# Splitting the first loads, adding filler matmuls in the opening, and turning the combine weights on VectorE in a fused attention and Soft-MoE kernel

## The chip, the cores and the metric

The kernel runs on one core of a Trainium2 chip. The metric is device time in microseconds (us) for one execution of the whole program, taken as a median of several runs. Lower is better. A core has TensorE (PE in the profile, with its weight loads as PEld), VectorE (DVE), ScalarE (ACT), GpSimd (POOL), and SyncE (SP), which here does nothing but issue transfers.

## The reference

The kernel computes two layers. The first is attention with 4 batches, 8 heads, 768 positions and head size 64, in which a query sees a key only where both fall into the same hash bucket. The bucket is given by the signs of six random projections.

```python
q_bits = einsum(q, proj) > 0          # 6 bits per query, the same for keys
mask   = bucket(q) == bucket(k)
scores = where(mask, q @ k.T / sqrt(64), -1e9)
attn   = exp(scores - scores.max(-1)); attn /= attn.sum(-1) + 1e-9
x      = (attn @ v) as [3072, 512]
```

The second is a Soft-MoE layer with 8 experts of 4 slots each, hidden size 1024.

```python
logits     = x @ phi                              # [3072, 32]
d          = softmax over the 3072 positions;  slot_input = d.T @ x
h          = relu(slot_input[e] @ w1[e]);      slot_out[e] = h @ w2[e]
c          = softmax over the 32 slots
out        = c @ slot_out                         # [3072, 512]
```

Everything is float32; the weights `w1` and `w2` are 64 pieces of 512 KB, and the output is 12 pieces of 512 KB.

## The kernel before

**Attention, head by head.** Heads go in pairs that share a 128-row tile of raw values. `load` brings q and k of a pair, `bits` projects them on TensorE and `over` compares with zero on VectorE. `split_hi` and `split_lo` cut each raw value into a rounded high part (ScalarE) and a remainder. `spread_y`, `spread_l`, `spread_x` and `spread_bits` move all that by transfers into the two operand tiles of a head, `Ys` and `Xs`, which lie together in `XYs` and of which there are three sets. Rows 64 to 96 hold the bits, scaled so that a mismatch costs a huge penalty. For each head the twelve steps of `smax` (L424, with a maximum on VectorE at L430 or L427) find a row maximum; `shift` and `shift_rows` (L445 to L459) turn it and send it by a small transfer into a row of `XYs`; the twelve steps of `scores` (L471, with an exponential on ScalarE at L475) then compute the probabilities; `acc` sums them on GpSimd and `av` (L500) multiplies with v.

**Order.** The order on every engine is written out beforehand. Each step gets a time in slots, six slots to a head, from the table `STEADY`, or from `ONCE` where it differs; `at` puts the steps into a plan, and they are emitted in the order of their times. An engine's queue, and the queue of transfers on SP, follow this order strictly.

**Opening.** The first head has functions of its own. SP issues the keys of the first pair (L228), the small tables, the queries (L230), `cst`, and v. `keep_warm` multiplies ones on TensorE (L264). `first_bits` (L380 to L392) computes the bits of both sides, copies raw rows into `Ys[0]` on ScalarE and compares on VectorE (`first_over`, L358, four pieces of 384 columns). `spin` (L438) is a filler matmul after each `smax` group of head 0. It reads 96 rows of `Ys[0]`. GpSimd clears rows 64 to 96 of `XYs` (L289), computes the remainders of the first pairs (L327) and compares the second head's bits (`bits_rest`).

**End of attention.** The last two heads have single-head versions (`one_sum` to `one_put`) of the normalization. `batch_max` to `batch_slots` fold each batch into the running softmax over positions. `batch_weigh` and `batch_share` make the combine weights `c` of a batch in the tile `call`.

**Experts.** `hidden` (L911) multiplies with w1, `above_zero` and `turned` (L917 to L927) apply the ReLU and transpose, `model` (L993) multiplies with w2 into the PSUM tiles `po0`, `po1` and `po2`, and `split_out` cuts the result into high and low parts. The weights arrive through pools `wa`, `wb`, `wy`, `wp`, `wl` and `wc`, which take over the memory of earlier stages as `free_pp`, `free_yp`, `free_ap`, `free_lp` and `free_mp` give it back (L855 to L878), and then through `wa` again once `hidden` has used its pieces. They are issued on SP at L198 and L200.

**Combine weights.** For the last product they must lie with the slots in rows. L941 and L942 split them into high and low parts; `arrange` (L944) copies three tiles of 128 positions at a time into a layout repeated four times, with eight small copies split between VectorE and GpSimd (L950); `turn_weights` (L953) transposes the three tiles by matmuls with the identity (L956) and copies them out of PSUM (L957). This is done eight times, between the steps of `hidden` and `model`.

**Output.** `send` (L1004) multiplies for one quarter of the 512 columns (128 columns) and all 3072 positions, in three pieces of 1024 positions (L1015), copies each out of PSUM (L1017) and issues its 512 KB (L1018). The first two quarters are sent after half of `po1`, the third between the halves of `po2`, the last at the end.

## Time and profile before

| What | Value |
| --- | --- |
| Median of 3 runs (lowest to highest) | 479.42 us (478.81 to 479.83) |
| The profiled execution's own time | 479.94 us |
| Its span, first to last instruction | 478.2 us |
| Busy share of the span: PE, DVE, POOL, ACT | 97%, 77%, 69%, 52% |
| Mean granted TensorE clock | 0.975 |
| HBM read, written | 52.76 MB, 6.29 MB |

The span is what the trace covers; 1.7 us of the profiled execution's time lie around it. Busy shares are averages over stages with different limits, so the views by stretch of time and the chain of waits decide what a change in one place is worth. The granted clock is 1.00 at full speed and 0.50 at half.

### The profile page before, as it was taken

How to read it: one execution, taken by the hardware profiler on the slowest of the kernel's cores; microseconds unless marked ns; L12 is line 12 of the kernel's file. 1: busy time of each engine (PE TensorE's matmuls, PEld its weight loads, DVE VectorE, ACT ScalarE, POOL GpSimd, SP SyncE). 2: the span in 40 equal slices, each digit the busy share in tenths (PEclk: the TensorE clock that was granted, in tenths of full speed). 3: DMA queues.
4: the chain of work that ended last, by engine and by line, in shares of the span. 5: the costliest groups of instructions: out<-in, count | busy, mean ns of one | idle time of the engine just before them, and what ended most of it. 6: DMA issues, size and time to landing. Idle time of an engine off the chain costs nothing.

```text
span 478.2 us, 10753 instructions
## 1 busy us (share of the span) xinstructions
PE 462.6 (97%) x4012; PEld 294.8 (62%) x4012; DVE 369.3 (77%) x690; ACT 247.5 (52%) x465; POOL 331.1 (69%) x236
## 2 busy tenths in 40 slices
PE   7899999999999999999999999999999999989992
PEld 4466666666666666666656666666656666553581
DVE  5649798989888888889898989898989865563242
ACT  4354646464657555555655555555654545431241
POOL 7758777878785978787868787878589888502200
PEclk9589999999999999999999999999999999999997
DMA  6667677767665757777674868584868479899967
GB/s 152 168 169 172 170 157 242 159 186 162 192 156 156 179 170 170 230 174 225 164 232 122 220 171 219 167 207 137 202 194 197 136 177 336 318 381 391 408 273 298
DMA packets 39697, 99.71 MB, mean 209 GB/s; under 512 B 7422, under 2 KB 13708, under 8 KB 39644
## 3 DMA queue, kind: packets, MB, share of 16 engines
q1 hardware_dynamic: 39260, 98.16, 70.9%
q0 software_dynamic: 224, 0.47, 0.5%
q8 instruction: 32, 0.52, 0.4%
q10 hardware_dynamic: 160, 0.39, 0.3%
q14 instruction: 21, 0.17, 0.1%
HBM read 52.76 MB, written 6.29 MB: 123 GB/s over the span
## 4 chain that ended last, share of the span: by engine, by line
PE 91%; DMA 4%; DVE 1%; SPq 1%; issue 1%; ACT 1%; DVEq 0%; ACTq 0%
PE st L471 29%; PE av L500 25%; PE smx L424 16%; PE qh L911 3%; PE mi L363 3%; PE mi L512 2%; PE mi L563 2%; PE mi L528 2%; PE qs L993 2%; DMA w<-w 2%; DMA out<-w 1%; PE mi L548 1%; DMA stage<-qk 1%; PE mi L718 1%; PE mi L455 1%; PE qa L956 1%
## 5 line engine op out<-in xcount | busy, mean ns | idle before, releaser
L488 POOL TENSOR_TENSOR acc<-acc,pt 128x768 f32<-128x768 f32 x125 | 229.0, 1832 | 9.6
L475 ACT ACTIVATE pt<-st 128x512 f32<-128x512 f32 x288 | 164.2, 597 | 65.0 <-PE st L471 59.9
L471 PE MATMUL st<-XY 128*128 128x256 f32 (+1 forms) x768 | 179.4, 349 | 0.1
L430 DVE TENSOR_REDUCE mx<-smx 128x1 f32<-128x512 f32 x192 | 131.0, 688 | 30.2 <-PE smx L424 27.5
L471 PEld LDWEIGHTS st<-XY 128*128 128x128 f32 x768 | 126.9, 191 | 18.3 <-ACT pt L475 1.7
L500 PE MATMUL av<-pt,v 128*32 128x384 f32 x1536 | 133.0, 486 | 0.0
L424 PE MATMUL smx<-XY 96*128 96x256 f32 (+1 forms) x384 | 120.8, 365 | 0.8 <-DVE mx L430 0.4
L482 POOL TENSOR_TENSOR acc<-pt 128x768 f32<-128x768 f32 x32 | 58.9, 1840 | 59.9 <-ACT pt L475 59.8
L500 PEld LDWEIGHTS av<-pt,v 128*32 128x32 f32 x1536 | 49.4, 110 | 72.8 <-issue 71.6
L424 PEld LDWEIGHTS smx<-XY 96*128 96x128 f32 x384 | 68.3, 195 | 30.1 <-issue 9.8
L427 DVE TENSOR_REDUCE mx<-smx 128x2 f32<-128x512 f32 x96 | 65.8, 686 | 6.5 <-PE smx L424 5.8
L504 ACT COPY avs<-av 128x384 f32<-128x384 f32 x32 | 15.3, 477 | 90.6 <-PE av L500 90.6
L324 DVE TENSOR_REDUCE stage<-stage 128x768 fp32r<-128x1536 f32 x28 | 49.0, 1785 | 0.0
L520 DVE RECIPROCAL rs<-sm 128x128 f32<-128x128 f32 x45 | 38.6, 914 | 11.9 <-ACT sm L515 7.0
L317 ACT ACTIVATE stage<-stage 128x768 fp32r<-128x768 f32 x30 | 24.1, 837 | 3.1 <-DMA stage<-qk 2.7
L565 DVE TENSOR_TENSOR xq<-mi,r 128x256 f32<-128x256 f32 x45 | 17.4, 413 | 1.5 <-PE mi L563 1.5
L950 POOL CAST avs<-lacc 128x48 fp32r<-128x48 f32 x8 | 2.1, 266 | 19.5 <-ACT lacc L941 12.4
L993 PE MATMUL qs<-w 128*32 128x128 f32 (+1 forms) x360 | 15.5, 305 | 0.0
L563 PE MATMUL mi<-ident,avs 128*128 128x128 f32 x90 | 14.7, 272 | 0.0
L911 PE MATMUL qh<-w,siT 128*32 128x512 f32 x128 | 14.6, 595 | 0.0
L563 PEld LDWEIGHTS mi<-ident,avs 128*128 128x128 f32 x90 | 11.7, 140 | 4.0
L363 PE MATMUL mi<-stage,pb 128*32 128x384 f32 x120 | 13.4, 521 | 0.0
(179 smaller groups left out, 330.1 us busy)
## 6 DMA issues: line engine op xcount, KB each, us to landing
w<-w SPq DMA_DIRECT2D x61, 512.0 KB
XY<-stage SPq DMA_DIRECT2D x62, 384.0 KB
stage<-qk SPq DMA_DIRECT2D x32, 384.0 KB
XY<-stage SPq DMA_DIRECT2D x62, 192.0 KB
v<-vt SPq DMA_DIRECT2D x32, 192.0 KB
out<-w SPq DMA_DIRECT2D x12, 512.0 KB
xq<-w SPq DMA_DIRECT2D x3, 512.0 KB
XY<-bt SPq DMA_DIRECT2D x62, 19.5 KB
```

The source lines that it names most:

```text
L324: nc.vector.tensor_reduce(out=w[:, 2 * x + 1], in_=stage[:, x:n + 1:n - x].rearrange("p t s -> p s t"), axis=AX.X, op=ALU.add, negate=True)
L424: nc.tensor.matmul(pt[:, o:o + b - a], Ys[h % N_Y][0:96, 0, t * P:(t + 1) * P], Ys[h % N_Y][0:96, 1, a:b], start=True, stop=True)
L427: nc.vector.tensor_reduce(out=mx[:, n - 1:n + 1], in_=pt.rearrange("p (a x) -> p a x", a=2), axis=AX.X, op=ALU.max)
L430: nc.vector.reduce_max(out=mx[:, n:n + 1], in_=pt, axis=AX.X)
L471: nc.tensor.matmul(pt[:, o:o + b - a], x[:, 1, i * P:(i + 1) * P], x[:, 0, a:b], start=first, stop=not first)
L475: nc.scalar.activation(pts[i // 2][:, 512 * u:512 * u + 512], pt, AF.Exp, scale=D ** -0.5)
L482: nc.gpsimd.tensor_tensor(out=s["acc"], in0=pr[:, 0:S], in1=pr[:, S:2 * S], op=ALU.add)
L488: eng.tensor_tensor(out=s["acc"], in0=s["acc"], in1=pr[:, a * S:(a + 1) * S], op=ALU.add)
L500: nc.tensor.matmul(s["av"][D * c + d:D * c + d + 32, 0:HC], s["v"][:, i, d:d + 32], pr[:, o + c * HC:o + (c + 1) * HC], start=(i == 0), st ...
L520: nc.vector.reciprocal(out=st[h]["rs"][:, k * P:(k + 1) * P], in_=st[h]["sm"][:, k * P:(k + 1) * P])
L563: nc.tensor.transpose(pt[:, o:o + P], st[h + a]["avs"][:, k * P:(k + 1) * P], ident)
L911: nc.tensor.matmul(ph[fh][32 * j:32 * j + 32], siT[:, k, 4 * g + j, :], wt[0, g, k, j][:, fh * 512:(fh + 1) * 512], start=(k == 0), stop=( ...
```

## The change

It has five parts.

1. **Raw values in halves.** The small table is loaded first; then the first 64 rows (head 0) of keys and queries, then the other 64 rows (head 1). The bits of head 0 are computed from its half alone, and `first_over` works in five pieces (512 columns once, 256 four times) instead of four of 384. The bits of both heads are computed again from all 128 rows (`more_bits`) for head 1. The second pair is loaded into the tiles `accs[1]` and `accs[2]`, early in the opening, and its `split_hi` and `bits` are early too. `cst` comes later. VectorE clears rows 64 to 96 of `Ys[0]` and a part of `Ys[2]`; GpSimd clears the rest and writes the row of ones directly, where transfers did it.
2. **Fillers.** `keep_warm` at the start becomes `spin(7)`, with 128 rows and 512 columns of a constant. Head 0's `smax` steps, but for the last tile of rows, are each followed by two (part 0) or one (part 1) fillers of 448 columns, 15 in all, where there were 9 of 512; six further steps `spin` of two fillers of 512 columns stand in the plan of the opening.
3. **Combine weights.** `batch_share` writes a high part and a remainder into a larger `call`. `combine` turns them by VectorE's 32 by 32 transpose, reading each block twice for the repeated layout: 16 instructions for each of three parts of 10, 8 and 6 tiles. `combine_round` copies a part on ScalarE. The first part stands in the plan beside heads 30 and 31, the second behind the first `hidden`, the third behind the second `turned`. `arrange`, `turn_weights` and the 24 matmuls with the identity are gone. The slot order of `phi`, `fold` and `siT` changes to suit.
4. **Outputs.** The first two quarters are sent in thirds, each third between parts of `po1`; the third quarter in two parts around the last half of `po2`.
5. **Pools and order.** `wb` has 7 buffers (5), `wy` 3 (6), `wc` 2 (1), and one more piece goes into the buffer of the first combine part. Scratch of `pair_rec` shares the buffer `dl`. All times in `STEADY` and `ONCE` are new, with separate entries for the first heads and for heads 29 to 31.

```diff
-N_WA, N_WB, N_WY, N_WP, N_WL, N_WC = 23, 5, 6, 3, 5, 1
+N_WA, N_WB, N_WY, N_WP, N_WL, N_WC = 23, 7, 3, 3, 5, 2
...
+    def raws(h, x):
+        return accs[1 + x] if h == 2 else raw[:, x]
...
+    def load_half(a):
+        for x in (1, 0):
+            nc.sync.dma_start(out=raw[D * a:D * a + D, x], in_=qk[x, 0, D * a:D * a + D])
...
-    load(0, (1,))
     nc.sync.dma_start(out=pre[:, 0:C_ID + 64], in_=first[:, 0:C_ID + 64])
-    load(0, (0,))
-    nc.sync.dma_start(out=pre[:, C_ID + 64:], in_=cst[:, C_ID:C_FD])
+    load_half(0)
+    load_half(1)
...
-    keep_warm(7, True)
+    def spin(n, cols=512):
+        pt = p_av.tile([P, 512], F32, name="av")
+        for _ in range(n):
+            nc.tensor.matmul(pt[:, 0:cols], idle[:, 0:P], idle[:, P:P + cols], start=True, stop=True)
+
+    spin(7)
...
+    nc.vector.memset(Ys[0][64:96].bitcast(F32), 0.0)
+    nc.vector.memset(Ys[2][64:96, 0].bitcast(F32), 0.0)
...
     def first_rows(i):
+        ts = XYs[i] if i else Xs[0]
+        if i == 2:
+            nc.gpsimd.memset(Xs[2][64:96, 0].bitcast(F32), 0.0)
+        nc.gpsimd.memset((ts[64:96, 1] if i == 2 else ts[64:96]).bitcast(F32), 0.0)
+        nc.gpsimd.memset(ts[ROW:ROW + 1, 1].bitcast(F32), 1.0)
...
+    def first_copy(x):
+        nc.scalar.copy(Ys[0][0:64, x], raw[0:64, x])
+
+    def first_bits(x):
+        first_pt[x] = p_st.tile([P, 512], F32, name="st")
+        for c, (a, b) in enumerate(((0, 512), (512, S))):
+            j = 2 * x + c
+            nc.tensor.matmul(first_pt[x][32 * j:32 * j + 32, 0:b - a], pb[0:D, 32 * x:32 * x + 32], raw[0:D, x, a:b],
+                             start=True, stop=True)
+
+    def more_bits():
+        pt = p_mi.tile([P, 512], F32, name="mi")
+        for x in range(2):
+            bits_of(0, x, pt)
+        st[0]["bt"] = st[1]["bt"] = pp.tile([P, HC], F32R, name="bt", bufs=1)
+        nc.scalar.copy(pts[0][:, 0:HC], pt[:, 0:HC])
...
-        if h == 0 and n % 4 != 1:
-            spin(1)
+        if h == 0 and t < NT - 1:
+            spin(2 - part, 448)
...
+        nc.scalar.copy(hb, cb)
+        eng.tensor_tensor(out=cb.bitcast(F32R), in0=cb, in1=hb, op=ALU.subtract)
+
+    cuts = 0, 10, 18, B * NT
+
+    def combine(n, j, q):
+        t0, t1 = cuts[n:n + 2]
...
+        src = tiles[32 * q:32 * q + 32, o:o + t1 - t0, j]
+        nc.vector.transpose(out=turned_shares[n][32 * j:32 * j + 32].rearrange("r (t q k) -> r t q k", q=4, k=32)[:, :, q],
+                            in_=src[:, :, None].broadcast_to([32, t1 - t0, 2, 4 * SPE]))
+
+    def combine_round(n):
...
+        nc.scalar.copy(cts[n // 2][:, o:o + t.shape[1]], t)
...
-    batch_weigh(B - 1)
-    batch_share(B - 1)
     ps_stack.close()
...
     hidden(hid[0], 0, range(KC))
+    batch_weigh(B - 1)
+    combine_some(1, 0, 8)
+    batch_share(B - 1)
+    combine_some(1, 8, 12)
     load_weights(wa, 10)
     hs0, hT0 = above_zero(hid[0])
-    cts = [piece().bitcast(F32R) for _ in range(B)]
     hidden(hid[1], 1, range(1))
     turned(hs0, hT0)
-    for k in range(1, KC):
-        hidden(hid[1], 1, range(k, k + 1))
-        more_weights(1)
+    combine_some(1, 12, 16)
+    combine_round(1)
+    hidden(hid[1], 1, range(1, KC))
...
     turned(hs1, hT1)
+    combine_some(2, 0, 16)
+    combine_round(2)
     model(po0, 0, 0, range(4, FC))
-    more_weights(1)
-    model(po0, 0, 1, range(4))
-    more_weights(1)
-    model(po0, 0, 1, range(4, FC))
+    model(po0, 0, 1)
     so0 = split_out(po0, 0)
-    more_weights(1)
     model(po1, 1, 0, range(4), left)
-    more_weights(1)
-    model(po1, 1, 0, range(4, FC), left)
-    more_weights(1)
-    send(so0[:, left], 0)
-    send(so0[:, right], 1)
-    model(po1, 1, 1, cols=left)
+    for n in range(3):
+        send(so0[:, left], 0, (n,))
+        send(so0[:, right], 1, (n,))
+        if n < 2:
+            model(po1, 1, n, range(4 - 4 * n, FC), left)
     so1 = split_out(po1, 1, left)
     po2 = po_tile(P)
     model(po2, 1, 0, cols=right)
-    send(so1, 2)
+    send(so1, 2, (0, 1))
     model(po2, 1, 1, cols=right)
-    send(split_out(po2, 1, right), 3)
+    so2 = split_out(po2, 1, right)
+    send(so1, 2, (2,))
+    send(so2, 3)
```

The new plan emits the opening in this order (steps of one kind drawn together): `first_bits(1)`, `first_copy(1)`, `first_hi(1)`, `load(2)`, `first_bits(0)`, `first_hi(0)`, `first_copy(0)`, the five `first_over` with `more_bits` and two `spin` steps among them, `spread_y(1)`, `split_hi(2)`, head 0's twelve `smax` with two `spin` steps among the last, `shift(0)`, `copy_ident`, `spin`, `bits(2)`, `spin`, `shift_rows(0)`, ten `smax` steps of head 1, and then the first `scores` of head 0. Before, six `smax` steps of head 1 had stood ahead of the first `scores`. Near the end of attention, `av(31, 0)` now stands ahead of `one_log`, `one_sum` and `one_turn` of head 30, which it followed before.

More of the change, by code (lines that the diff above doesn't have):

```diff
@@ new lines @@
+    ('scores', 1, 3, 0): 7.365414, ('scores', 1, 3, 1): 9.323528, ('scores', 1, 4, 0): 9.600144,
+    ('scores', 1, 4, 1): 8.023727, ('scores', 1, 5, 0): 8.410207, ('scores', 1, 5, 1): 7.791596,
+    ('shift', 0): -4.033776, ('shift', 1): 2.601141, ('shift_rows', 0): -2.144996, ('shift_rows', 1): 3.53153,
+    ('smax', 0, 0, 0): -6.352233, ('smax', 0, 0, 1): -8.6847, ('smax', 0, 1, 0): -8.289554,
+    ('smax', 0, 1, 1): -5.236389, ('smax', 0, 2, 0): -4.693721, ('smax', 0, 2, 1): -6.335023,
+    ('smax', 0, 3, 0): -5.871465, ('smax', 0, 3, 1): -9.069782, ('smax', 0, 4, 0): -9.552866,
@@ new lines @@
+    ('scores', 7, 2, 0): 42.260896, ('scores', 9, 2, 0): 54.260896, ('shift', 0): -26.571425,
+    ('shift', 1): 2.981046, ('shift', 2): 9.041854, ('shift', 31): 182.981046, ('shift_rows', 0): -15.952961,
+    ('shift_rows', 1): 4.460206, ('shift_rows', 2): 9.51256, ('shift_rows', 30): 177.51256,
+    ('shift_rows', 31): 184.460206, ('smax', 0, 0, 0): -69.826587, ('smax', 0, 0, 1): -59.319775,
+    ('smax', 0, 1, 0): -55.407906, ('smax', 0, 1, 1): -42.16177, ('smax', 0, 2, 0): -66.791397,
+    ('smax', 0, 2, 1): -55.145618, ('smax', 0, 3, 0): -52.669685, ('smax', 0, 3, 1): -36.552905,
@@ L220, in lsh_attention_soft_moe @@
     nc.vector.memset(ones, 1.0)
-    idle = pts[2][:, 0:P]
-    nc.vector.memset(idle, 1.0)
+    XYs = [held.tile([P, 2, 2, S], F32R, name=f"XY{i}") for i, held in enumerate((yp, lp, yq))]
+    Xs, Ys = [[t[:, :, n] for t in XYs] for n in range(2)]
+    idle = Xs[2][:, 0, 0:P + 512]
+    nc.vector.memset(idle.bitcast(F32), 1.0)
     eps = cp.tile([P, 1], F32, name="eps")
@@ L355, in first_x, with over @@
         nc.scalar.copy(Xs[0][0:64, x], st[0]["w4"][0:64, 3 * x])
-    def over(out, pt, rows, eng=nc.vector):
-        eng.tensor_scalar(out=out, in0=pt[rows, 0:HC], scalar1=con[rows, C_TH:C_TH + 1],
+    def over(out, pt, rows, eng=nc.vector, cols=slice(0, HC)):
+        eng.tensor_scalar(out=out, in0=pt[rows, cols], scalar1=con[rows, C_TH:C_TH + 1],
                           scalar2=con[rows, C_AM:C_AM + 1], op0=ALU.is_gt, op1=ALU.mult)
@@ L783, in at @@
         plan.append((when, len(plan), (f, *args)))
[L785 to L789 removed]
+    for i in range(N_Y):
         at(first_rows, i)
@@ L792, in lsh_attention_soft_moe @@
     at(load_phi)
-    at(keep_warm, 3, True, tag="a")
+    at(load_cst)
     at(copy_ident)
-    at(first_bits)
-    at(first_last)
+    for n in (1, 0):
+        at(first_copy, n)
+        at(first_bits, n)
+        at(first_hi, n)
+    for xab in ((1, 0, 512), (0, 0, 256), (1, 512, S), (0, 256, 512), (0, 512, S)):
+        at(first_over, *xab)
+    at(more_bits)
+    for n in range(6):
+        at(spin, 2, tag=n)
     at(bits_rest)
@@ L848, in lsh_attention_soft_moe @@
     at(keep_warm, 10, tag="c")
+    for j in range(4):
+        for q in range(4):
+            at(combine, 0, j, q)
+    at(combine_round, 0)
     last = NT * BH
```

351 lines of the change are left out of this document (171 added, 180 removed), and 5 rows, old and new, of the table ONCE.

## The prediction

> **What bounds the kernel now.** I read the page first: engine shares and the two rows over 40 slices.
>
> ```profile
> PE 462.6 (97%) x4012; PEld 294.8 (62%) x4012; DVE 369.3 (77%) x690; ACT 247.5 (52%) x465; POOL 331.1 (69%) x236
> ...
> PEclk9589999999999999999999999999999999999997
> DMA  6667677767665757777674868584868479899967
> ```
>
> TensorE sets the time nearly everywhere. Two places differ: the opening, where its clock is down, and the end, where the transfers are full. For the opening I cut the windows view into equal stretches on whose borders the clock changes (columns: us, busy and instructions of PE, PEld, DVE, ACT, POOL, clock, DMA share, GB/s).
>
> ```profile
> 4.14:7.55 3.41, 2.45 (x15) 0.94 (x14) 2.27 (x5) 2.87 (x4) 1.11 (x3) 1.00 0.43 136
> 7.55:10.97 3.42, 2.25 (x9) 1.51 (x9) 2.60 (x5) 0.95 (x2) 3.33 (x5) 0.99 0.75 146
> 10.97:14.38 3.41, 3.41 (x10) 2.31 (x9) 2.79 (x5) 1.58 (x2) 3.35 (x4) 0.50 0.97 241
> ...
> 21.21:24.62 3.41, 3.22 (x7) 2.17 (x8) 2.54 (x4) 0.60 (x1) 0.25 (x1) 0.50 0.45 91
> 24.62:28.04 3.42, 3.42 (x12) 2.89 (x11) 1.66 (x4) 1.78 (x3) 0.00 (x0) 0.51 0.96 304
> ```
>
> After stretches only 2.45 and 2.25 us busy, the clock falls to half at 10.97 and comes back at 28.04. The stretch from 10.97 is busy throughout and doesn't bring it back; that from 24.62 does. The first holds only matmuls of 96 rows (L424, L438), the second also `scores` of 128 rows. The chain of waits has one 512-column step at half and at full clock:
>
> ```profile
> 12.40 0.43 PE smx L424
> ...
> 40.65 0.23 PE smx L424
> ```
>
> At the end the windows view shows the transfers:
>
> ```profile
> 435.00:455.00 20.00, 20.00 (x257) 10.11 (x246) 5.12 (x24) 5.17 (x11) 3.61 (x20) 1.00 1.02 409
> ...
> 455.00:460.00 5.00, 5.00 (x66) 3.94 (x54) 2.45 (x5) 3.17 (x7) 0.00 (x0) 1.00 0.27 106
> 460.00:474.00 14.00, 9.02 (x210) 7.55 (x208) 5.97 (x11) 4.57 (x10) 0.00 (x0) 0.92 1.02 401
> ```
>
> From 435 to 455 weights fill them at 409 GB/s, from 460 outputs at 401. Between, 5 x (1 - 0.27) = 3.65 us of transfer time is lost: the weights are in and no output is ready. So the end is bound by transfers; what TensorE saves there counts only as far as it closes this hole.
>
> **Opening, term by term.** The timeline of the opening:
>
> ```profile
> 1.12 0.48 DVE L233 MEMSET phs<- 128x512 f32 x1
> ...
> 3.88 0.83 ACT L386 CAST XY<-stage 64x768 fp32r<-64x768 f32 x1 [1.65 <-DMA stage<-qk]
> 4.08 0.23 DVE L241 TENSOR_TENSOR pb<-pt 128x64 f32<-128x64 f32 x1 [2.48 <-DMA pt<-first]
> ...
> 5.32 1.38 DVE L358 TENSOR_SCALAR XY<-st,con 16x384 fp32r<-16x384 f32 x2 [0.93 <-PE st L363]
> ...
> 6.00 0.84 PE L363 MATMUL st<-stage,pb 128*32 128x384 f32 x4 [0.80 <-DMA stage<-qk]
> ...
> 8.65 3.58 POOL L327 TENSOR_TENSOR stage<-stage 128x768 fp32r<-128x768 f32 x2
> ...
> 10.43 1.29 DVE L430 TENSOR_REDUCE mx<-smx 128x1 f32<-128x512 f32 x2
> ...
> 12.38 1.65 POOL L358 TENSOR_SCALAR bt<-pt,con 128x384 fp32r<-128x384 f32 x1
> ...
> 14.09 2.69 POOL L289 MEMSET XY<- 32x1536 f32 x2
> ...
> 15.42 0.69 DVE L427 TENSOR_REDUCE mx<-smx 128x2 f32<-128x512 f32 x1 [0.16 <-PE smx L424]
> ...
> 16.63 0.17 DVE L448 SCALAR_TENSOR_TENSOR mz<-mi,mz 128x6 f32<-128x6 f32 x1
> ...
> 22.52 1.05 PE L471 MATMUL st<-XY 128*128 128x512 f32 x2
> ```
>
> Both sides' raw values are in at 6.00. Head 0's half behind the small table is about as much as had landed by 4.08, so I take 4.3; VectorE then becomes what everything waits for. Its chain: the table (first in the queue, 65 KB) lands between 2 and 4.08, say 3.0; L241 and its neighbour, 0.4; clearing 1536 and 768 columns at 0.48 per 512, 2.2: 5.6. Comparing 1536 columns at 0.69 per 384, and one instruction more: 2.9, to 8.5. Nine maxima at 0.65: 14.4. `shift` as now (from the last maximum's end near 16.1 to 16.8): 0.7. So `shift` ends at 15.1 instead of 16.80. GpSimd must be through before: 4.2 for clearing (2.69 per 3072 columns, and the row of ones), 2.3 for `Xs[0]`, `bits_rest` 1.65, two remainders 3.6, with waits about 14.0; the cover is 1.1 us, and whatever is over it delays `shift_rows`. Two 384 KB loads of the second pair pass `spread_y(1)` and `cst` in SP's queue; at the rates of the windows some 3 us, and neither is needed before 14.
>
> `shift_rows` stands ahead of ten `smax` steps of head 1 (seven groups), then the first `scores`. VectorE compares `bits(2)` (0.69) and must finish five maxima (3.3) before TensorE can pass the seventh: 15.1 + 0.7 + 3.3 + 0.5 for the matmuls = 19.6 against 22.52. **2.9 us.** From there the old kernel stays at half clock to 28.04: 5.5 us in which it does 2.76 us of work. **2.76 us** if the clock holds. Together 5.66; I take **-5.5**. The fillers cost nothing at full clock: a `smax` step and two fillers are 0.23 x (512 + 896) / 512 = 0.63 us, beside a maximum of 0.65. Bounds: -2.5 if the clock falls back for part of it, -6.5 if the table lands at 2.
>
> The Trainium skill, TensorE: Matmul & The Clock Gate, Part 1 (the HAM clock gate), says that a busy stretch of about 3.4 us releases the clock and an idle one takes it back. By that rule the stretch from 10.97 should have released it; the rows say no, so busy time alone doesn't decide here. By the rule the clock would hold in the new opening, which is never idle, and the sum stays as it is; the rows leave room for the first rival.
>
> **End, term by term.** `turn_weights` goes; the chain of waits has its pieces and the others I use:
>
> ```profile
> 409.39 0.77 PE mi L616 x4
> ...
> 411.82 0.33 PE mi L591 x3
> ...
> 436.30 1.02 PE qa L925 x8
> ...
> 439.18 0.48 PE qa L956 x3
> ...
> 454.25 1.01 PE qs L993 x32
> ```
>
> Eight times 0.48 = 3.84 us leave TensorE, and one half of a `model` (1.01) moves behind the first output. The timeline:
>
> ```profile
> 427.17 0.49 DVE L896 COPY siT<-mi 128x128 f32<-128x128 f32 x2 [0.54 <-PE mi L892]
> ...
> 428.74 0.35 DVE L765 TENSOR_REDUCE cs<-call 128x6 f32<-128x192 f32 x1 [0.43 <-ACT call L759]
> ...
> 433.80 0.69 DVE L917 TENSOR_SCALAR w<-qh 128x512 f32<-128x512 f32 x1 [1.38 <-PE qh L911]
> ...
> 458.40 13.57 SPq L1018 DMA_DIRECT2D out<-w  x12
> ```
>
> The first output is issued at 458.40 - 3.84 - 1.01 = 453.55, before the weights end (about 455.45). The hole closes: **-3.65**. The pools hold one piece less when memory is waited for (`wy`): one more 512 KB behind that wait, 512 KB / 409 GB/s = **+1.28**. That memory comes free 0.77 + 0.33 earlier, as `av(31, 0)` passes `one_log` and `one_turn`: **-1.1**. Sum **-3.5**, between -1.5 (the last term nothing, the hole half closed) and -4.75 (the second nothing). Twelve outputs at 1.31 us each follow the weights; the five buffers and the pieces of `model` between them (about 2 us) are shorter than the four outputs then in flight (5.2), so thirds keep the transfers fed.
>
> **The transposes on VectorE** are not in the trace. Nearest rows:
>
> ```profile
> L430 DVE TENSOR_REDUCE mx<-smx 128x1 f32<-128x512 f32 x192 | 131.0, 688 | 30.2 <-PE smx L424 27.5
> ...
> L520 DVE RECIPROCAL rs<-sm 128x128 f32<-128x128 f32 x45 | 38.6, 914 | 11.9 <-ACT sm L515 7.0 <-POOL acc L488 4.9
> ```
>
> 256 columns cost 0.34 at the maximum's rate, 1.83 at the reciprocal's. I take 0.4: like the maximum, one pass over its input. The second part puts 12 of them and six steps of some 0.35 between 427.66 and L917, which must start by 436.3 - 0.69: room for 5.8 / 12 = 0.49 each, so they are covered. If that is gone, the next cover is the queue of weights: the first output may be 456.7 - 453.55 = 3.2 us late, which lasts to about 0.67 us each. The Trainium skill, VectorE: DVE Perf Modes, The three transpose paths, gives 311 ns for 128 bf16 columns; as an estimate from this page twice that is 0.62 for 256, which by my sum would still be covered. The first part (16 of about 0.45, 7.2 us) goes into this window, where VectorE idles 12.2 us:
>
> ```profile
> 380.00:410.00 30.00, 30.00 (x244) 19.61 (x236) 17.77 (x37) 16.35 (x31) 25.47 (x15) 1.00 0.84 267
> ```
>
> `combine_round` and the added copies and subtractions of three batches lie on ScalarE and GpSimd, beside full TensorE or transfers.
>
> **The repeated order** is new in every entry, with the same work. Pairs start with these pieces of the chain:
>
> ```profile
> 42.71 3.87 PE av L500 x48
> ...
> 67.42 3.87 PE av L500 x48
> ...
> 91.78 3.87 PE av L500 x48
> ```
>
> Two neighbouring pairs of one kernel differ by 24.71 - 24.36 = 0.35. A new order could shift each of 15 pairs by perhaps a quarter of that either way: 0, +-1.5.
>
> **Sum.** 479.94 (a span of 478.2 and 1.74 around it) - 5.5 - 3.5 + 0 = 470.9. The profiled execution is 0.52 above the median of 479.42, so the forecast is **470.4**, its own range 467.5 to 472.5.
>
> **Rivals.** *The clock falls back.* Between 15.5 and 19.6 TensorE has only 0.23 us of 96-row work per 0.65 us, less than in the stretch after which it fell. `Scores` would then run at half until a full stretch is over, some 5 us: +2.5, **472.9**. Against it: the stretches ahead are full, and one of 2.45 us busy was survived.
>
> *The fillers at half clock.* If constants, like the 96-row matmuls from 10.97, don't count as activity, the opening is TensorE-bound at half clock. Head 0's `smax` (4608 columns), 15 fillers (6720) and four of 512 make 13,376 columns, 11.2 us at 0.43 per 512, from about 7.95 (second halves in at some 5.5, then two `first_hi` and `first_copy(0)` on ScalarE, 0.83 each as at 3.88): the last maximum ends at 19.8, `shift` at 20.5, 3.7 late, and nothing comes back: 479.42 + 3.7 - 3.5 = **479.6**, no gain. Against it: the fillers use 128 rows, as did the stretch that worked.
>
> *The transposes hold TensorE up.* This ends slower. At the reciprocal's 1.83 the second part ends 12 x (1.83 - 0.49) = 16 us late, the third (16 of 1.37 us beside 7 us of `model`) 15 more; less the 3.2 us of cover, 470.4 + 28 = **498**. It starts to cost at 0.67 us per 256 columns and eats the gain at 24d = 25, d = 1.05. For it speaks only that 32-column blocks are written with gaps; against it that no row but the reciprocal is that slow.
>
> *More from the order* than 1.5 us: below 466.5.
>
> **Chances.** Forecast 0.64, clock falls back 0.18, fillers at half 0.06, transposes 0.05, more from the order 0.07. The range 466.5 to 475.5 holds the first two and their bounds; the others are 0.18. A difference of 0.2% (0.96 us) is what a measurement can tell: faster 0.89 (first, second, last), within it 0.03 (half of the filler case), slower 0.08.
>
> **What would show it.** Right: clock 1.00 from some 4 to 8 us on, first `scores` near 19.6, no hole before the outputs, transposes of 0.3 to 0.5 us, pairs of 24.3 us. Wrong: half clock after 12 us; TensorE waiting for VectorE at the turn of the first ReLU; outputs not following the weights at once; pairs over 24.5 us.

## The result: slower by 1.2%, and the profile after

The changed kernel takes 485.30 us (median of 4 runs, 482.80 to 486.54); the kernel before took 479.14 us beside it (4 runs, 478.81 to 479.83). The ratio is 1.0120, with a 95% interval of 1.0098 to 1.0142. The forecast was 470.4 us, 9 us faster than before. Runs more than 1.5% above the fastest of their kernel are left out of all ratios here and below. The profiled execution took 484.93 us with a span of 483.1 us, so 4.9 us of span have to be found (483.1 - 478.2).

The page of the changed kernel, with the rows that answer to those quoted of before:

```profile
PE 463.2 (96%) x3997; PEld 291.6 (60%) x3997; DVE 389.3 (81%) x708; ACT 247.8 (51%) x461; POOL 327.3 (68%) x204
...
PEclk9999999999999999999999999999999999999997
```

TensorE works 0.6 us more than before and stands idle 4.3 us more (19.9 against 15.6 us). VectorE works 20 us more; the 48 turns alone take 21.4 us. The clock row looks better than before from its first digit on, but a stretch without a record of the clock is shown as full, and the durations tell otherwise.

**Opening.** The chain of waits of the changed kernel (start, duration in us, what), then its timeline:

```profile
1.63 3.35 PE av L338 x7
4.98 1.87 PE st L450 x5
...
10.01 1.22 PE av L338 x2
...
12.41 0.43 PE smx L489
...
18.34 0.24 PE smx L489
...
32.38 1.73 PE av L559 x17
```

```profile
5.23 0.70 DVE L349 MEMSET XY<- 32x768 f32 x1
...
6.88 3.09 DVE L421 TENSOR_SCALAR XY<-st,con 16x512 fp32r<-16x512 f32 x5 [0.95 <-PE st L450]
...
16.44 0.69 DVE L492 TENSOR_REDUCE mx<-smx 128x2 f32<-128x512 f32 x1 [0.57 <-PE smx L489]
...
21.75 0.16 DVE L507 SCALAR_TENSOR_TENSOR mz<-mi,mz 128x6 f32<-128x6 f32 x1
...
26.47 0.63 PE L530 MATMUL st<-XY 128*128 128x512 f32 x2
```

A `smax` step of 512 columns takes 0.43 us at 12.41 and 0.24 us at 18.34: TensorE was at half clock until some 14 us. Until 4.98 it is in the seven first fillers, and the first head's bits come behind them (L450), so VectorE's comparisons start at 6.88. The first `smax` step waits for two planned fillers (10.01). From then on VectorE waits for TensorE ahead of eight of the nine maxima (0.57 us at 16.44): they take from 11.70 to 21.23 us, 9.5 us instead of the 5.9 of the forecast. `shift` ends at 21.9 and the first `scores` come at 26.47, 3.95 us later than before. From there the clock is full, and at the first `av` the lateness has fallen to 1.2 us (32.38 against 31.15).

**Repeated part.** The chain of the changed kernel at pairs 3 to 6, and below it the same pairs of the kernel before:

```profile
168.06 3.87 PE av L559 x48
...
179.16 6.57 DMA XY<-mr
...
193.85 3.87 PE av L559 x48
...
204.94 6.64 DMA XY<-mr
...
219.70 3.87 PE av L559 x48
...
230.78 6.27 DMA XY<-mr
...
245.16 3.87 PE av L559 x48
...
371.41 3.87 PE av L559 x48
```

```profile
166.80 3.87 PE av L500 x48
191.18 3.87 PE av L500 x48
...
239.89 3.87 PE av L500 x48
...
365.73 3.87 PE av L500 x48
```

The lateness is 1.26 us at 168, and 5.27 us at 245: three pairs in a row take 25.5 to 25.9 us instead of 24.4. In each of them the chain runs through the small transfer that brings a head's row of maxima into `XYs`, and the waits of TensorE from 160 to 330 us (sum, times, longest) are these three:

```profile
PE st L530 <- DMA XY<-mr: 3.7, 3, 1.4
```

SP's queue ahead of the first of these rows, and below it ahead of the same row in the kernel before:

```profile
173.06 0.51 SPq L255 DMA_DIRECT2D w<-w  x1
173.67 0.37 SPq L366 DMA_DIRECT2D v<-vt  x1
174.14 0.84 SPq L271 DMA_DIRECT2D stage<-qk  x2
175.04 1.41 SPq L394 DMA_DIRECT2D XY<-stage  x2
179.16 0.82 SPq L394 DMA_DIRECT2D XY<-mr  x1
```

```profile
171.21 0.51 SPq L303 DMA_DIRECT2D v<-vt  x1
171.77 0.42 SPq L198 DMA_DIRECT2D w<-w  x1
172.30 0.83 SPq L211 DMA_DIRECT2D stage<-qk  x2
177.14 0.76 SPq L331 DMA_DIRECT2D XY<-mr  x1
```

A weight, a value load and two raw loads stand ahead of the row in both; the two moves (`XY<-stage`) stand ahead of it only in the new order.

The last pair of the list is 5.68 us late. So 4.4 us come from here.

**End.** The windows view (us, busy and instructions of PE, PEld, DVE, ACT, POOL, clock, DMA share, GB/s), and the issue of the outputs in the timeline:

```profile
440.00:460.00 20.00, 18.48 (x256) 8.90 (x248) 13.46 (x33) 3.76 (x6) 0.00 (x0) 1.00 1.03 409
460.00:464.00 4.00, 2.22 (x37) 1.57 (x37) 1.84 (x4) 2.17 (x4) 0.00 (x0) 1.00 0.47 182
464.00:482.00 18.00, 11.31 (x216) 8.73 (x216) 7.04 (x12) 5.85 (x12) 0.00 (x0) 0.90 0.89 352
```

```profile
453.96 6.12 DVE L846 STREAM_TRANSPOSE w<-call 32x192 f32<-32x192 f32 x16
...
463.16 14.19 SPq L1083 DMA_DIRECT2D out<-w  x12
```

The hole in the transfers between weights and outputs is still 4 x (1 - 0.47) = 2.1 us wide (3.65 before), and the outputs run at 352 GB/s instead of 401. The third part of the turns ends at 460.08; the rounding, the cut of the result and the first products follow, and the first output is issued at 463.16. The end as a whole gains 4.9 - 5.68 = -0.8 us.

Opening +1.3, order +4.4, end -0.8: that is the 4.9 us.

### The profile page after: what moved, and what is told of

Read it like the earlier page. It is cut to its first block, busy times and chain, and to the rows that moved or that the text cites. A ratio compares the mean times of both kernels' runs of the same rounds, so it can differ in the third digit from the quotient of the medians.

```text
span 483.1 us, 10622 instructions
## 1 busy us (share of the span) xinstructions
PE 463.2 (96%) x3997; PEld 291.6 (60%) x3997; DVE 389.3 (81%) x708; ACT 247.8 (51%) x461; POOL 327.3 (68%) x204
## 4 chain that ended last, share of the span: by engine, by line
PE 75%; DMA 14%; DVE 5%; POOL 3%; issue 1%; ACT 1%; SPq 0%; DVEq 0%; POOLq 0%; ACTq 0%
PE st L530 25%; PE av L559 20%; PE smx L489 14%; DMA XY<-mr 4%; DMA w<-w 4%; DMA XY<-stage 3%; PE av L338 3%; PE mi L426 2%; PE mi L622 2%; POOL acc L547 2%; PE mi L571 2%; DMA xq<-w 2%; PE qs L1058 1%; PE mi L587 1%; DVE mx L495 1%
## 5 line engine op out<-in xcount | busy, mean ns | idle before, releaser
L530 PE MATMUL st<-XY 128*128 128x512 f32 (+1 forms) x768 | 179.7, 343 | 3.8 <-DMA XY<-mr 3.7
L530 PEld LDWEIGHTS st<-XY 128*128 128x128 f32 x768 | 128.6, 190 | 21.4 <-DMA XY<-stage 4.5
L489 PE MATMUL smx<-XY 96*128 96x512 f32 (+1 forms) x384 | 123.5, 362 | 1.5 <-DVE mx L492 0.7
L489 PEld LDWEIGHTS smx<-XY 96*128 96x128 f32 x384 | 67.2, 189 | 31.9 <-issue 8.1
L579 DVE RECIPROCAL dl<-sm 128x128 f32<-128x128 f32 x45 | 38.8, 916 | 11.9 <-ACT sm L574 11.9
L624 DVE TENSOR_TENSOR xq<-mi,r 128x256 f32<-128x256 f32 x45 | 17.6, 418 | 0.0
L338 PE MATMUL av<-XY 128*128 128x512 f32 (+1 forms) x34 | 15.0, 533 | 1.7 <-DVE eps L290 1.6
L1058 PE MATMUL qs<-w 128*32 128x128 f32 (+1 forms) x352 | 15.1, 303 | 0.0
L846 DVE STREAM_TRANSPOSE w<-call 32x256 f32<-32x256 f32 (+1 forms) x32 | 12.9, 403 | 1.6 <-PE qh L1010 1.2
L517 ACT CAST mr<-mi 12x128 fp32r<-12x128 f32 x32 | 7.6, 239 | 11.8 <-PE mi L514 11.8
```

Of the source, the lines that this page charges most:

```text
L338: nc.tensor.matmul(pt[:, 0:cols], idle[:, 0:P], idle[:, P:P + cols], start=True, stop=True)
L489: nc.tensor.matmul(pt[:, o:o + b - a], Ys[h % N_Y][0:96, 0, t * P:(t + 1) * P], Ys[h % N_Y][0:96, 1, a:b], start=True, stop=True)
L530: nc.tensor.matmul(pt[:, o:o + b - a], x[:, 1, i * P:(i + 1) * P], x[:, 0, a:b], start=first, stop=not first)
L579: nc.vector.reciprocal(out=st[h]["rs"][:, k * P:(k + 1) * P], in_=st[h]["sm"][:, k * P:(k + 1) * P])
```

## The experiments

One measure serves all of them: when ScalarE copies a head's row of maxima (`mr<-mi`, `shift_rows`), against the same copy in the profile of the kernel before. A lateness that stays the same over the heads was made earlier; one that grows was made there. The ratio is to runs of the kernel before beside each kernel. All but the ratio comes from one profiled execution, which can lie far from the median (488.60 us in order_of_before, 488.22 in weights_of_before). fillers_96 and opening_even, whose runs lie 8 us and more apart, are told below.

| Kernel | Ratio (95% interval) | Head 1 | Head 13 | Head 22 | Head 30 | Head 31 | Span |
| --- | --- | --- | --- | --- | --- | --- | --- |
| changed | 1.0120 (1.0098 to 1.0142) | +1.4 | +2.0 | +6.4 | +6.2 | +7.7 | +4.9 |
| order_of_before | 1.0123 (1.0074 to 1.0172) | +2.5 | +5.7 | +5.7 | +8.4 | +9.7 | +8.6 |
| weights_of_before | 1.0115 (1.0059 to 1.0171) | +1.0 | +2.0 | +5.1 | +8.4 | +9.4 | +8.2 |
| old_order_all | 1.0034 (1.0011 to 1.0058) | +1.5 | +1.6 | +1.8 | +2.2 | +4.3 | +2.2 |
| warm_first | 1.0075 (1.0052 to 1.0098) | -0.1 | +0.5 | +1.6 | +3.0 | +4.1 | +2.9 |
| opening_new_order | 1.0311 (1.0271 to 1.0352) | +12.5 | +15.8 | +15.7 | +15.7 | +15.7 | +15.3 |
| opening_old_order | 1.0225 (1.0181 to 1.0270) | +6.8 | +6.8 | +6.9 | +6.9 | +6.8 | +6.5 |
| opening_dense | 1.0053 (1.0026 to 1.0081) | +1.0 | +1.3 | +1.4 | +1.3 | +1.4 | +0.9 |
| opening_dense_long | 1.0056 (1.0037 to 1.0075) | +2.8 | +2.5 | +2.6 | +2.5 | +2.5 | +2.3 |
| opening_light | 0.9977 (0.9959 to 0.9996) | -1.1 | -1.2 | -1.3 | -1.3 | -1.3 | -1.5 |
| tail_alone | 1.0021 (0.9995 to 1.0048) | +0.2 | +1.2 | +1.8 | +2.0 | +4.2 | +1.9 |
| tail_earlier | 0.9989 (0.9966 to 1.0012) | -0.5 | -0.4 | -0.4 | -0.1 | +2.0 | -1.6 |
| tail_spread | 0.9980 (0.9965 to 0.9994) | +0.1 | +0.8 | +0.8 | +1.1 | +1.0 | -1.3 |
| tail_round | 0.9946 (0.9926 to 0.9965) | -0.2 | +0.2 | +0.3 | +0.7 | +2.1 | -1.6 |
| both | 0.9932 (0.9919 to 0.9945) | -0.8 | -1.1 | -0.8 | -0.7 | -0.7 | -3.9 |
| both_later | 0.9942 (0.9922 to 0.9963) | -2.2 | -1.9 | -2.0 | -1.3 | -1.3 | -4.0 |

### The order of the heads

Both tables stand in the kernel, and each step takes its time from one of them:

```diff
-        when = ONCE.get(key)
+        before = 5 <= tag < 17 if f is load_weights else f in steps_of_heads and 4 <= ints[0] < 28
+        steady, once = (STEADY_B, ONCE_B) if before else (STEADY, ONCE)
+        when = once.get(key)
```

> The changed kernel, with the old order for every step of the heads 4 to 27 and for the weight loads 5 to 16; opening and end stay changed. Theory (queue order): the pairs that start at 193.85, 219.70 and 245.16 us lose 1.3 us each because the move of the maxima's row stands behind a weight, a value load, a raw load and two moves in SP's queue. With the old order those waits on the row go, and the 4.1 us that the repeated part lost come back: 485.3 - 4.1 = 481.2 us. Rival (phase): the waits come from the later start that the new opening leaves to every transfer; then they stay, and the time is 484.5 to 485.5.

The time didn't fall: 485.41 us. But the rows separate what happened. Pairs of the old order in its chain:

```profile
172.51 3.87 PE av L637 x48
...
245.51 3.87 PE av L637 x48
```

These three pairs take 24.3 us each, and the lateness is 5.7 us from head 13 to head 22, where the changed kernel goes from 2.0 to 6.4. So the three waits are gone. Two passages from one order to the other ate that: +3.2 us between heads 1 and 13 (made between heads 2 and 6), +2.7 us between heads 22 and 30 (made between heads 26 and 28).

Then the weight loads alone:

```diff
+        before = f is load_weights and 5 <= tag < 17
```

> The changed kernel, with the old order for the weight loads 5 to 16 alone. Theory (a 512 KB weight just ahead of the row's move delays it): at least 3 of the 4.1 us come back, 481.2 to 482.3 us. Rival (the raw load and the two low-half moves, which the new order puts ahead of the row's move, do it without the weight): the waits on the row stay near 8 us in sum and the time within 1 us of 485.3.

486.57 us, the median of four runs between 482.43 and 489.76, too far apart to decide by themselves. TensorE's waits between 160 and 330 us still hold this row, the same sum as in the changed kernel, at other pairs:

```profile
PE st L608 <- DMA XY<-mr: 3.7, 3, 1.9
```

The rival's forecast came out, but the edit didn't ask the question. It shifted weights, and none away from the late rows: the chain runs through the rows issued at 203.56, 280.20 and 305.81 us, and a weight was issued 4.8 to 5.3 us ahead of each (198.77, 275.19, 300.52), followed by the same value load, raw loads and moves as in the changed kernel. That a weight ahead of the row is not enough is seen in the kernel before (171.77 and 177.14 above), whose chain runs through no such row. Which of the transfers delays it was not taken apart; the two moves are what the queue has more.

The clean test puts the old times to every step from the first shift on, to the end:

```diff
 STEADY = {
-    ('acc', 0, 0): 2.625835, ('acc', 0, 1): 3.878658, ('acc', 0, 2): 5.139808, ('acc', 1, 0): 8.045214,
+    ('acc', 0, 0): 4.5212609, ('acc', 0, 1): 4.97490753, ('acc', 0, 2): 5.24282413, ('acc', 1, 0): 7.49131977,
...
```

> The changed kernel with its opening and its end, but with the old order from the first shift on, for all heads. Theory (the new order of the heads costs 4 to 5 us by late rows of maxima; passages between two orders cost 2 to 3 us each in order_of_before): no head after the first pair loses against the kernel before, and the time is 480.5 to 482 us against 485.3 of the changed kernel. Rival (the order is worth nothing either way and the runs only differ): 484 to 486 us.

481.42 us, as the theory had it. The ratio falls from 1.0120 to 1.0034, 0.0086 x 479.4 = 4.1 us, and from head 1 to head 30 only 0.7 us are lost. The new order costs some 4 us; the two intervals together leave 2.6 to 5.7.

### The opening

First the old first fillers in the changed kernel:

```diff
-    idle = Xs[2][:, 0, 0:P + 512]
-    nc.vector.memset(idle.bitcast(F32), 1.0)
+    still = pts[2][:, 0:P]
+    nc.vector.memset(still, 1.0)
...
-    spin(7)
+    keep_warm(7, True)
```

> The changed kernel, with one edit: the first filler is the old one, seven small products of 32 output rows, which start after a clearing of 128 columns instead of 640. Theory (the first fillers start too late for the clock's first stretch): the clock is full from about 4 us, the first smax step comes near 8.5 instead of 11.03 us, the first scores near 21.5 instead of 26.47, and the time is 485.3 - 5 = 480.3 us. Rival (too little work behind the first fillers, or constants do not count): the clock falls back or is not released before 10 us, the first scores come at 25 us or later and the time is 484 to 485.5 us.

The median of the eight runs in the ratio is 483.12 us (two more took 579.24 and 988.29 us). In the profile a `smax` step takes 0.23 us from the first one at 9.54 on, so the clock was full; the first `scores` came at 23.68. Neither theory had that: the clock is right and 3 us are still missing. Two rows of its timeline, on GpSimd and on TensorE, show one place:

```profile
19.77 0.73 POOL L359 MEMSET XY<- 32x768 f32 x1 [3.08 <-PE mi L516]
```

```profile
27.48 0.36 PE L491 MATMUL smx<-XY 96*128 96x256 f32 x1 [1.06 <-DMA XY<-bt]
```

The fillers read the third `XYs` tile, so GpSimd can't set that tile's rows before the last filler is through; the bits for it go out late and TensorE waits 1.06 us. The maxima come at the same slow pace as is shown below for opening_dense.

Which products keep the clock? The same kernel with fillers of 96 rows:

```diff
-            nc.tensor.matmul(pt[:, 0:cols], idle[:, 0:P], idle[:, P:P + cols], start=True, stop=True)
+            nc.tensor.matmul(pt[:, 0:cols], idle[0:96, 0:P], idle[0:96, P:P + cols], start=True, stop=True)
```

> warm_first with fillers that read 96 of their 128 rows, so that no product between the small table and the first scores uses all rows but the small ones. Theory (rows count: products of 96 rows do not keep the clock): the clock falls to half between 11 and 15 us, the first scores come at 26 us or later, 486 us. Rival (busy time alone decides): clock full from about 5 us on, as in warm_first, 483.5 us.

Two runs, 494.27 and 483.83 us, and the profile is of the longer one. In it a `smax` step still takes 0.43 us at 22.81, where warm_first, which differs in nothing but the fillers' rows, had 0.23 from 9.54 on. But the other run is as fast as those of warm_first, so the two don't show that fillers of 96 rows lose the clock. The next two kernels change the fillers further. They are the kernel before with the changed opening, fewer and smaller fillers that read another tile, and no planned fillers:

```diff
-        if h == 0 and t < NT - 1:
-            spin(2 - part, 448)
+        if h == 0 and t < NT - 1 or h == 1 and ("st", 0, 0) not in st[0]:
+            keep_warm(1, True)
...
-    for n in range(6):
-        at(spin, 2, tag=n)
```

> The kernel before with the changed opening, mended: the first filler is the old one, the six pairs of fillers of the plan are gone, one small product of the first filler's kind follows each smax step of head 0 and those of head 1 ahead of the first scores, and no filler reads the third XY tile. Heads 0 to 3 in the new order, all later ones and the end as before. Theory (the opening's gain is there once the clock is released early and the fillers neither hold TensorE up nor keep GpSimd from the third tile's rows): clock full from about 4.5 us, first smax near 8.5, first scores near 20, everything later 3 to 4 us earlier than before: 475.5 to 476.5 us. Rival (the clock falls back with fewer fillers): first scores near 22, 479 to 480 us. Rival (the passage from one order to the other costs): 480 us or more with a full clock.

> As opening_new_order, but from the first shift on in the old order. Theory (the gain lies in the opening alone): 475 to 476.5 us. If the passage between the two orders costs something, this one is at least 1 us faster than opening_new_order; if the new order of heads 0 to 3 is worth something, it is slower. Rival (the clock falls back): 479 to 480 us.

493.67 and 488.70 us. Both profiles stand at half clock for long. A window of opening_old_order:

```profile
18.60:35.60 17.00, 17.00 (x46) 9.16 (x46) 7.10 (x13) 4.71 (x8) 3.35 (x3) 0.50 0.35 99
```

TensorE is busy for all of 17 us and stays at half, so busy time alone doesn't release the clock here either. In opening_new_order a `smax` step of 512 columns still takes 0.63 us in the timeline at 37.52, against 0.39 at 41.86; the same first fillers after which the clock was full at 4.14 us in the kernel before didn't release it here. Old against new order of the first heads can't be told from these two, as their clocks differ; but opening_new_order gains another 3.3 us of lateness between heads 1 and 13 with its passage to the old order, and opening_old_order, without one, none.

So the full fillers again, with nine first ones, in one kernel, and fifteen in the next:

```diff
-    keep_warm(7, True)
+    keep_warm(9, True)
...
-        if h == 0 and t < NT - 1 or h == 1 and ("st", 0, 0) not in st[0]:
-            keep_warm(1, True)
+        if h == 0 and t < NT - 1:
+            spin(2 - part, 448)
+        elif h == 1 and ("st", 0, 0) not in st[0]:
+            keep_warm(2, True)
```

> opening_old_order (the kernel before with the changed opening and the old order from the first shift on) with nine instead of seven first fillers, the changed kernel's fillers of 448 columns behind the smax steps of head 0, two small ones behind each smax step of head 1 ahead of the first scores, and the third tile's rows set behind head 2's first remainder. Theory (the gain is there if the clock holds): clock full from 5 to 8 us on without a gap, first scores near 21 us, 2 to 3 us earlier throughout than the kernel before: 476.5 to 478 us. Rival (where the stretches of the clock fall against the fillers is chance): a clock released only at 11 us or later in the profile, and times spread over 4 us or more.

> opening_dense with fifteen first fillers, 6.9 us of small products of full height at half clock, so that a whole stretch of 3.41 us lies in them wherever the stretches begin. Theory (one such stretch releases the clock): clock full by 8 us at the latest in every run, times within 2 us of each other, all of it some 2 us later than opening_dense at its best: 478 to 480 us. Rival (small products of 32 output rows do not release it by themselves): clock at half until 11 us or later, 481 us or more.

opening_dense: 481.11 us, seven of its ten runs within 480.87 and 481.54, the longest 487.82. opening_dense_long: 482.27 to 482.55 us in its four runs. A first filler of 6.08 us, longer than a stretch of the clock, makes the opening repeatable in these four runs, as the theory had it; the time is 2.4 us above the upper end of its forecast. And opening_dense refutes its own forecast: its profile has a full clock through the whole opening, and it is still 1.0 us late at head 1. From its timeline:

```profile
13.09 0.69 DVE L676 TENSOR_REDUCE mx<-smx 128x2 f32<-128x512 f32 x1 [0.57 <-PE smx L673]
...
23.09 0.62 PE L517 MATMUL av<-pt,ones 128*32 128x128 f32 x4
23.64 0.73 PE L716 MATMUL st<-XY 128*128 128x512 f32 x2
```

At full clock VectorE still waits 0.57 us for each maximum over two steps of 256 columns: with their three fillers they take 1.26 us of TensorE. `shift` ends at 17.6. And each of the six steps ahead of the first `scores` carries 0.62 us of small fillers. What the clock gives, the fillers take.

Two ways to take less: no fillers behind head 1's steps, or one filler behind each step of head 0 and a small one instead of two behind head 1's. Both also move one cast of head 0 (`first_x(1)`) ahead, and what that alone is worth was not run.

```diff
-        elif h == 1 and ("st", 0, 0) not in st[0]:
-            keep_warm(2, True)
```

> opening_dense without the small fillers behind head 1's smax steps, and with head 0's second cast ahead of its moves. Theory (the nine fillers of 0.62 us between 18 and 27 us take what the full clock gives): first scores near 22 instead of 23.64 us, the second row of maxima 3 us earlier, 478 us where the clock holds. Rival (the clock falls back between 18 and 23 us, where only maxima and products of 96 rows are left): 481 to 483 us with half clock for 6.8 us or more.

```diff
-            spin(2 - part, 448)
-        elif h == 1 and ("st", 0, 0) not in st[0]:
-            keep_warm(2, True)
+            spin(1, 448)
+        elif h == 1 and not begun:
+            keep_warm(1, True)
```

> opening_dense with one filler of 448 columns behind every smax step of head 0 (two or one before), and one small filler instead of two behind head 1's steps, ahead of the very first scores alone. Theory (TensorE's period of 1.26 us for two steps of 256 columns, against 0.69 us of the maximum, falls to 0.95, so that VectorE sets the pace): the first shift 1 us earlier, first scores near 21 us, 476.5 to 478 us. Rival (so few fillers do not hold the clock): half clock somewhere between 8 and 25 us, 481 us or more.

opening_light is the first opening that gains: 478.61 us (ratio 0.9977, 1.1 us), head 1 1.1 us early and every later one 1.2 to 1.3. Its first `scores` start at 22.32, and that although the clock fell twice for a stretch:

```profile
8.80:12.10 3.30, 3.30 (x9) 2.48 (x10) 2.06 (x4) 1.77 (x3) 2.82 (x2) 0.50 0.66 152
...
22.50:25.80 3.30, 3.30 (x9) 2.73 (x10) 1.75 (x3) 1.19 (x2) 0.10 (x1) 0.51 0.30 72
```

opening_even falls into two groups, six runs from 476.24 to 480.23 us and four from 484.31 to 484.66. Its profile is of the second group:

```profile
8.70:32.50 23.80, 23.52 (x63) 13.37 (x64) 13.38 (x22) 5.57 (x11) 12.47 (x9) 0.50 0.51 128
```

With one filler to a step the clock can stay at half for 24 us. The median of the faster group is 477.9 us, within the forecast for a clock that holds; no profile of that group was taken, so that the clock makes the difference is not shown.

### The end

The kernel before with parts 3 to 5 of the change, without the new times of the heads:

```diff
-N_WA, N_WB, N_WY, N_WP, N_WL, N_WC = 23, 5, 6, 3, 5, 1
+N_WA, N_WB, N_WY, N_WP, N_WL, N_WC = 23, 7, 3, 3, 5, 2
...
+    for j in range(4):
+        for q in range(4):
+            at(combine, 0, j, q)
+    at(combine_round, 0)
```

> The kernel before with the changed end alone (combine weights turned by VectorE in three parts, thirds, pools); opening and order of the heads as before. Theory (new steps on VectorE late in the chain): the turned slots stand about 1.5 us later than before, the last outputs 1 to 2 us earlier against them: 478.5 to 479.5 us, no gain. Rival (the 1.5 us come from the new order of heads 29 to 31): the turned slots stand where they were and 2 us are gained, 477 us. The prediction's own end term would give 475.9 us.

481.63 us, no gain. Head 30's row is 2.0 us late in this run, and head 31's 4.2. The waits of TensorE around it:

```profile
PE smx L442 <- DVE mx L445: 1.2, 1, 1.2
```

Turns of the first part stand among head 31's maxima. What makes head 30's row 2.0 us late, ahead of the first turn at 393.63, is not shown. The third part first:

```diff
+    combine_some(2, 0, 6)
     hs1, hT1 = above_zero(hid[1])
+    combine_some(2, 6, 12)
...
-    combine_some(2, 0, 16)
+    combine_some(2, 12, 16)
     combine_round(2)
```

> tail_alone with the third part of the turns moved: six ahead of the ReLU of the second half, six between it and the copy that follows, four where all sixteen were. Theory (the last sixteen turns and the rounding behind them are what the first output waits for): the first output leaves 1.5 us earlier and the time falls from 481.6 to 480.1 us. Rival (the outputs are paced by TensorE's products between them, whatever the first one does): no change, 481 to 482 us.

478.44 us. The hole is gone:

```profile
455.00:460.00 5.00, 4.86 (x97) 3.52 (x94) 2.78 (x5) 2.15 (x4) 0.00 (x0) 1.00 1.02 407
```

The time fell more than forecast, but head 30 was 2.1 us earlier in this profile than in that of tail_alone, and so were the heads long before the moved turns; against head 30's row the span gains 1.5 us instead of 0.1. Now the first part:

```diff
-    ('combine', 0, 0, 0): 183.379315854,
+    ('combine', 0, 0, 0): 179.160,
...
-    ('combine_round', 0): 193.46702426,
+    ('combine_round', 0): 189.3,
```

> tail_earlier with the first part's sixteen turns moved into four gaps of VectorE: four before the tenth group of head 31's maxima, four behind its shift, four behind the division for heads 28 and 29, four behind the copies of their values, and the rounding ahead of head 30's sums. Theory (head 31's row of maxima comes 2 us late because twelve of the turns stand among its maxima, and memory for the last weights comes free that much later): the row comes as in the kernel before, the weights end 2 us earlier and so do the outputs: 478.4 - 2 = 476.5 us. Rival (the late row costs nothing, since the transfers are full from 417 us on): 478 to 479 us.

479.06 us, 0.2% faster than before. Head 31's row is now no later than head 30's, and against head 30 the span gains 2.4 us. The time is still 2.6 us above the forecast of 476.5. There is a new wait, between 380 and 425 us:

```profile
PE mi L609 <- ACT sm L602: 1.5, 1, 1.5
```

The rounding of 1.26 us on ScalarE, which I had put earlier, holds up a copy for TensorE. So it moves again:

```diff
-    ('combine_round', 0): 189.3,
+    ('combine_round', 0): 190.9,
```

> tail_spread with the rounding of the first part behind ScalarE's last exponentials instead of ahead of head 30's sums. Theory (the rounding of 1.26 us on ScalarE holds up the copy for which TensorE waits 1.47 us, and with it the memory of the last weights): the wait goes, the weights end 1.5 us earlier against the heads: 477.5 us. Rival (the stream of weights has 1.5 us of its own to make up elsewhere): 479 us, as tail_spread.

476.85 us, ratio 0.9946. The wait is gone and the gain over the kernel before is 2.6 us. The profiled execution (478.42 us) is one of the longer ones: its span is only 0.3 us shorter than that of tail_spread, and in it TensorE waits 1.2 us for head 31's maxima. So the runs show the gain, and no profile shows all of it.

### Both

> The changed kernel with the opening of opening_light, the end of tail_round and the old order from the first shift on. Theory (they add): heads 1.2 us earlier than in the kernel before, the end 2.6 us shorter: 479.5 - 3.8 = 475.7 us. Rival (the end is a stream of transfers that starts when memory is free and takes what the opening gives): 476.9 us, as tail_round.

> both, with one instead of four turns among head 31's maxima; two of the other three go behind the first copies of heads 28 and 29, one more behind the last. Theory (the row of head 31 and the memory behind it come 1.2 us earlier): 1 us faster than both, 474.7 us. Rival (the transfers have slack there, or the turns hold up others where they went): within 0.5 us of both.

The changed kernel with the opening of opening_light, the end of tail_round and the old order takes 475.85 us, ratio 0.9932: 3.3 us faster than before, where 1.1 and 2.6 us were seen one by one. They add, but for 0.4 us. both_later moves three turns,

```diff
-    ('combine', 0, 0, 1): 179.161,
+    ('combine', 0, 0, 1): 182.77,
...
```

and takes 476.08 us: no difference, as its rival had it. In both the outputs follow the weights without a hole; in the profile of both the first is issued at 453.44:

```profile
450.00:455.00 5.00, 4.87 (x92) 3.46 (x84) 2.04 (x4) 1.49 (x4) 0.00 (x0) 1.00 1.02 402
```

## Why the prediction was wrong, step by step

**What bounds the kernel** was right: TensorE nearly everywhere, transfers at the end. What came of each step on that ground was not. Forecast were -5.5 us for the opening, 0 for the order and -3.5 for the end; the profile shows +1.3, +4.4 and -0.8.

**The opening** is the largest miss, 6.8 us. Two steps failed. The first is the clock: "clock 1.00 from some 4 to 8 us on" was the ground of the sum, and it was at half until some 14 us. The second is **"so `shift` ends at 15.1"**, which it missed by 6.8 us: the maxima began at 11.70 instead of 8.5 and took 9.5 us instead of 5.9. VectorE's own chain was about right: it was through with its clearing at 5.9 us for a forecast of 5.6. Left out of the sum were the first fillers, behind which the first bits stand, and the six planned ones (the first `smax` step waits for two of them). The clock is not all of it: opening_dense, with a full clock throughout, has `shift` end at 17.6.

**"The fillers cost nothing at full clock"** failed with it. The 0.63 us were worked out from columns alone, for a step of 512 columns with two fillers. But three of the nine maxima wait for two steps of 256 columns with three fillers: 1856 columns, 0.83 us at 0.23 us for 512 and so already more than the maximum's 0.69. They take 1.26 us, about 0.09 us more for each of the five products. Each of them has its own weights to load (the page counts as many weight loads as products); that the 0.09 us lie there is not shown.

**"0, +-1.5" for the repeated order** failed by more than its range: 4.1 us by old_order_all, 4.4 in the profile. I took it for noise around the old pair, and called the range from the difference of two neighbouring pairs. What the runs showed in its place is a wait of TensorE for three rows of maxima, 3.7 us in sum, where the old order has none. A full TensorE hides how close each wait is. The queue of transfers stood in the tables; I went through it for the opening and not for the pairs.

**"2.76 us if the clock holds"** was right where it did: the lateness falls by 2.7 us between the first `scores` and the first `av` of the changed kernel.

**The rival of fillers at half clock** came nearest: forecast 20.5 us for the end of `shift`, measured 21.9. That is in part luck. It had the `smax` steps start at 7.95 us and the clock stay at half to the end of them; they started at 11.03 and the clock rose at some 14 us. Its ground, that constants don't count, is not shown: the stretch that ends with the rise holds fillers of 128 rows and steps of 96. Why the first seven fillers, 3.35 us of them, didn't release the clock stays open. The rival of a lull in which the clock falls back did not come about in the changed kernel's profile, but it did in that of opening_light.

**The end.** The turns cost what was forecast: 0.4 us for 256 columns, measured 0.45. The rival that they hold TensorE up for 16 us and more is refuted. That the hole closes (-3.65) is right in tail_earlier and wrong in the change: "the first output is issued at 453.55" charged the third part against the time of `model`, but it starts only after the copy behind the second ReLU, and 6.1 us of turns and a rounding stand behind that. The terms for memory (+1.28 and -1.1) left out that the first part's turns push head 31's maxima back. The bound of -1.5 doesn't follow from its own terms either: half the hole and no third term give -1.83 + 1.28 = -0.55, and the measured -0.8 lies within that. I had found 12.2 us of idle VectorE between 380 and 410, and an average over 30 us doesn't say that the gaps lie where the turns go.

## What to carry to other kernels

A filler is a user of TensorE, of its tile and of its place in the queue: cost it by the measured time of a step with its fillers, against the slowest partner of the loop, and look who wants to write the tile that it reads. Where an engine is full, the price of a reordering is not visible in its busy time; go through the transfer queue and ask for each small transfer that ends a wait what now stands ahead of it. Put added work of a side engine into gaps found in the timeline, not into a stretch whose busy share is low.

## What the runs showed of the hardware

Busy time alone does not say when the clock of TensorE is released. Products of 96 rows mixed with small ones (128 rows, 32 output rows), and from 25.94 us on with `scores` of 128 rows, kept it busy for 17.00 of 17 us at 0.50 (opening_old_order); 6.08 us of the small ones alone released it (the profile of opening_dense_long, whose four runs lie within 0.28 us). The changed kernel's first fillers, full height and 512 columns wide but only 3.35 us long, did not.

Rows don't decide it either. The prediction set the stretch from 10.97 us of the kernel before, busy throughout with products of 96 rows and not followed by full clock, against a later one with 128 rows. tail_spread has the same opening, and there a stretch as full of the same products is followed by full clock:

```profile
10.53:13.95 3.42, 3.42 (x10) 2.41 (x11) 2.57 (x4) 1.87 (x3) 3.36 (x4) 0.50 0.92 224
13.95:17.36 3.41, 2.19 (x9) 1.08 (x7) 3.08 (x7) 1.22 (x2) 3.41 (x4) 1.00 0.55 177
```

The Trainium skill, TensorE: Matmul & The Clock Gate, Part 1 (the HAM clock gate), has windows of 3.4 us that run free of the kernel; that agrees with the changes of the clock in these rows, 3.41 to 3.42 us apart, and with their falling at other times than in the kernel before, whose opening is the same. It speaks of a busy window as enough, and there the runs differ; what the clock counts stays open.

A stall in the middle of a kernel can be paid twice. In weights_of_before TensorE was busy 1.50 us of one stretch, and the next one ran at half:

```profile
310.39:313.80 3.41, 1.50 (x11) 1.15 (x8) 1.29 (x2) 1.57 (x3) 3.33 (x3) 0.98 0.50 116
313.80:317.22 3.42, 3.42 (x12) 2.69 (x11) 1.73 (x4) 1.45 (x3) 0.49 (x1) 0.52 0.96 204
```

VectorE's transpose of 32 by 32 blocks of float32 takes 0.38 us for 192 columns (16 in 6.12 us) and 0.51 for 320 (3 in 1.53 us of tail_earlier): some 0.19 us and 1 ns for each column.
